# Attention, then two gated MLPs, in one kernel: weight splitting begun later and thinner, fewer first-layer products a pair at first, first loads by two queues

## The chip, the cores and the metric

One core of one Trainium2 chip runs the whole program. The metric is the device time of one execution in microseconds (us). Engines are named as in the profile: PE (TensorE, matrix products and transposes), PEld (its weight loads), DVE (VectorE), ACT (ScalarE), POOL (GpSimd) and SP (SyncE, which issues DMAs).

## What is computed

```python
# q, k, v: (4, 8, 576, 64); M_prev: (4, 8, 64, 64); weights float64
scores = (q @ k.T) / 8, causal mask;  a = softmax(scores);  local = a @ v
q_p = phi(q)                                   # phi(x) = max(x, 0) + exp(min(x, 0))
mem_out = (q_p @ M_prev) / (q_p . z_prev + 1e-6)
g = sigmoid(beta)                              # per head
x = g * mem_out + (1 - g) * local              # -> (2304, 512)
x = (sigmoid(x @ w_gate) * (x @ w_val)) @ w_out   # 512 -> 1536 -> 512
out = ((x @ w_a) * (x @ w_b)) @ w_out2            # 512 -> 1536 -> 512
```

The six weight matrices come in as 64-bit floats. Every product is made of three fp32r products of split operands: high x high, high x low, low x high.

## The kernel before, in words

**Attention stage (to line 860).** Two heads make a pair; there are 16 pairs, four to each of the four batches. The loop of line 770 runs 18 times and overlaps pair `p` (scores, masked minimum, exponentials), `p+1` (loads and transposes of queries and keys) and `p-1`, `p-2` (sums, transposed probabilities, the product with the values). `load_q`, `load_k`, `load_v` and `load_z` issue DMAs, all on SP's queue. `cut_q` splits the queries of a pair into a high part (DVE) and a low part (POOL).

**First-layer products inside it.** While attention of later pairs runs, the first MLP's first four of twelve chunks are computed for batches 0 to 2 (`moe_a`): a batch has 48 calls of `M`, each of three 128x512 products into tiles named `m` (144 products). `M` does the next call if its input is cut and its weight is ready, or nothing. `Ms(k)` asks for `k` of them; a pair has twelve such places. `room` forces calls where a buffer must come free. What is left is done behind the loop (line 854).

**Weight splitting.** `w_piece` turns 128x512 64-bit numbers (tile `st`) into a high and a low fp32r part (tile `w`) in steps. DVE masks bits and builds parts, ACT shifts the exponent, POOL multiplies the high part. With `WPOOL` set, as in this stage, ACT also converts the low part and POOL also makes the low product (line 444); without it, as in the second stage, DVE does both (lines 434 and 448). `w_stream` runs over the pieces, each three steps; the attention stage has 15 pieces. `fill`, called four times a pair, takes one step from pair 1 on and two from pair 4 on.

**Second stage (from line 861).** PE's order is the program's; the other engines' orders are made by a scheduler, as are all orders of the attention stage. `gv` computes gate and value products of a chunk (tiles `gv`, 24 products), `outs` the output products (tile `mo`). The first block is batch 3 with all twelve chunks: five have their weights from the attention stage, the other seven are split on the way, then the second MLP's follow. New pools stand where the attention stage's pools were, so the first loads of weights here come behind the last store of `fin` (line 541) in SP's queue.

Of the kernel before, what the change touches and what calls it, by code (L numbers as in the profile page):

```python
# [19 lines left out]
def kernel(  # L20
# [16 lines left out]
    nc = tc.nc  # L37
    P = 128
    B, H, S, D = q.shape
    NPAIR = H // 2  # L40
# [14 lines left out]
    vec, act, pool, pe = nc.vector, nc.scalar, nc.gpsimd, nc.tensor  # L55
# [42 lines left out]
    def place(p):  # L98
        b, r = divmod(p, NPAIR)
        return b, 2 * r  # L100


    def load_rows(t, src, p):
        b, h = place(p)
        nc.sync.dma_start(
            out=t[:, 0], in_=src[b, h:h + 2, 0:P, :].rearrange("h p d -> p h d")
        )
        for e in H2:
            nc.sync.dma_start(
                out=t[:, 1:NB, e], in_=src[b, h + e, 64:S, :].rearrange("(i p) d -> p i d", p=P)  # L110
            )

    def load_q(p):
        st["qn", p] = at.tile([P, NB, 2, D], F32, tag="qn", name="qn", bufs=2)
        load_rows(st["qn", p], q, p)

    def load_k(p):

        st["kn", p] = at.tile([P, NB, 2, 2, D], F32, tag="kn", name="kn", bufs=1)
        for r in H2:  # L120
            load_rows(st["kn", p][:, :, :, r], k, p)
# [14 lines left out]
    def load_z(p):  # L136
        b, h = place(p)
        zb = at.tile([P, 2, D], F32, tag="zb", name="zb", bufs=1)
        nc.sync.dma_start(
            out=zb.rearrange("p h d -> p (h d)"),  # L140
            in_=z_prev[b:b + 1, h:h + 2].rearrange("o h d -> o (h d)").broadcast_to([P, 2 * D]),
        )
        st["zb", p] = zb
# [11 lines left out]
    def cut_q(p):  # L155

        t = at.tile([P, NB, 2, 2, D], F32R, tag="qc", name="qc", bufs=1)
        vec.tensor_copy(out=t[:, :, :, 0], in_=st["qn", p])
        pool.tensor_tensor(
            out=t[:, :, :, 1], in0=st["qn", p], in1=t[:, :, :, 0].bitcast(F32), op=ALU.subtract  # L160
        )
        st["qc", p] = t
# [238 lines left out]
    def w_piece(wsrc, layer, c, kind, src):  # L401
# [24 lines left out]
        )  # L426
        if WPOOL:
            act.activation(out=low.bitcast(F32), in_=low, func=AF.Copy, scale=2.0 ** -20)
# [13 lines left out]
        )  # L442
        if WPOOL:
            pool.tensor_tensor(
# [10 lines left out]
    def w_stream(pieces, ahead):  # L455

        gens = []
        pieces = iter(pieces)

        def more():  # L460
            a = next(pieces, None)
            if a is not None:
                g = w_piece(*a)
                next(g)
                gens.append(g)

        for _ in range(ahead):
            more()
        yield
        while gens:  # L470
            g = gens.pop(0)
            for i in range(3):
                next(g)
                if i == 2:
                    more()
                yield
# [210 lines left out]
    NST, NG, NW = 2, MA, 1  # L687
    CD = "q"
    EDVE = ""
    WPOOL = True  # L690
    if True:
        start()
        wst = w_stream(
# [7 lines left out]
        def settle():  # L701
            while deferred:
                deferred.pop(0)()

        def M():

            settle()
            if not cur:
                if not batches:
                    return False  # L710
                cur.append(moe_a(batches.pop(0)))
                cur.append(next(cur[0]))
            b, key, f, after = cur[1]
            if b not in cut_a or key not in ws:
                return False
            with tc.issue_after(st["anchor"].ins):
                f()
            if after:
                deferred.append(after)
            nx = next(cur[0], None)  # L720
            if nx is None:
                cur.clear()
            else:
                cur[1] = nx
            return True

        def Ms(k=1):
            for _ in range(k):
                M()

        def split(k):
            while k and split_q and split_q[0][0] <= done[0] and split_q[0][3] <= len(finished):
                _, f, a, _ = split_q.pop(0)
                f(*a)
                if a[-1] == KD - 1:
                    cut_a.append(a[0])
                k -= 1

        def fill(p):
            settle()  # L740
            split(1)
            if p >= 1:
                with tc.issue_after(st["pace"].ins):
                    for _ in range(1 if p < 4 else 2):
                        next(wst, None)

        def room(p):

            old = divmod(p - 4, NPAIR)
            while any(x[1] is split_a and x[2] == old for x in split_q):  # L750
                split(1)
                if not M():
                    next(wst, None)
# [4 lines left out]
        for kk in range(KD):  # L758
            split_q.append((NPAIR * (B - 1) + kk + 1, split_last, (kk,), B - 1))

        load_q(0)
        load_k(0)
        load_z(0)
        load_v(0)
        cut_q(0)
        for e in H2:
            turn(0, e, "k")
            turn(0, e, "q")
            turn4(0, e)
        for p in range(NP + 2):  # L770
# [14 lines left out]
            if new:  # L785
                scores(p, 0, X_)
                expo(p, 0, X_)
            Ms()
            if last is not None:
                pv(last, Y_)  # L790
            Ms()
            if old is not None:
                turn_w(old, 1, "B")
                turn_w(old, 1, "C")
            Ms()
            fill(p)

            if new:
# [10 lines left out]
            if nx:  # L809
                cut_q(nx)  # L810
            Ms(2)
            fill(p)

            if new:
# [15 lines left out]
            if old is not None:  # L830
                for name in "01Y":
                    turn_mix(old, name)
            fill(p)

            if new:
# [25 lines left out]
    with tc.manual_schedule(engines={mybir.EngineType.PE}):  # L861
# [6 lines left out]
        NST, NG, NW = 2, 2, 1  # L868
        WPOOL = False
        wst = w_stream(  # L870
# [82 lines left out]
```

## Time and profile before

| what | value |
|---|---|
| median of 3 runs | 1192.5 us |
| lowest, highest | 1192.28, 1196.33 us |
| the profiled execution | 1195.14 us, span 1193.4 us |
| mean granted clock of TensorE | 0.986 |
| PE busy in the span | 96% |
| DVE, ACT, POOL busy in the span | 46%, 37%, 37% |

The span runs from the first to the last instruction; 1.7 us lie around it. Busy time of an engine is the time in which at least one of its instructions runs. Matmul ends are modelled, so that a busy PE can still run below its peak. The attention stage ends near 358 us, with the first `gv` product. "Pair p" below is the stretch from its first score product on PE to that of the next pair. Line numbers in rows of before are those of the kernel before; the changed kernel's are higher by one from line 106 on, and by more at the end.

### The profile page before, as it was taken

How to read it: one execution, taken by the hardware profiler on the slowest of the kernel's cores; microseconds unless marked ns; L12 is line 12 of the kernel's file. 1: busy time of each engine (PE TensorE's matmuls, PEld its weight loads, DVE VectorE, ACT ScalarE, POOL GpSimd, SP SyncE). 2: the span in 40 equal slices, each digit the busy share in tenths (PEclk: the TensorE clock that was granted, in tenths of full speed). 3: DMA queues.
4: the chain of work that ended last, by engine and by line, in shares of the span. 5: the costliest groups of instructions: out<-in, count | busy, mean ns of one | idle time of the engine just before them, and what ended most of it. 6: DMA issues, size and time to landing. Idle time of an engine off the chain costs nothing. (4 is left out here: it accounts for less than half of the span.)

```text
span 1193.4 us, 16159 instructions
## 1 busy us (share of the span) xinstructions
PE 1143.5 (96%) x6088; PEld 935.5 (78%) x6088; DVE 554.2 (46%) x1215; ACT 441.7 (37%) x967; POOL 435.8 (37%) x387
## 2 busy tenths in 40 slices
PE   6889999999999988989999998999999999999998
PEld 5667777787878867978888886888888888888897
DVE  6899988655636777860110678731100100200111
ACT  5877767777743223231211223222111211211121
POOL 5777776453413554431111344421111111111111
PEclk9999999999999999989999998999999999999999
DMA  7454543342114334331020433400200100100000
GB/s 170 109 155 104 132 117 109 80 108 75 48 47 152 106 113 163 118 119 53 8 99 1 165 118 124 142 18 1 71 1 1 71 1 1 36 18 1 1 37 18
DMA packets 129406, 89.66 MB, mean 75 GB/s; under 512 B 90032, under 2 KB 117680, under 8 KB 128432
## 3 DMA queue, kind: packets, MB, share of 16 engines
q1 hardware_dynamic: 129328, 88.63, 25.5%
q8 instruction: 48, 0.79, 0.3%
q14 instruction: 30, 0.25, 0.1%
HBM read 71.31 MB, written 17.30 MB: 74 GB/s over the span
## 5 line engine op out<-in xcount | busy, mean ns | idle before, releaser
L562 POOL TENSOR_TENSOR gl<-sg,gh 128x512 fp32r<-128x512 f32 (+1 forms) x120 | 149.2, 1244 | 502.1 <-ACT gh L149 474.1
L479 PE MATMUL gv<-xh,w 128*128 128x512 f32 (+1 forms) x864 | 321.1, 372 | 7.2 <-ACT xh L615 4.2
L480 PE MATMUL gv<-xl,w 128*128 128x512 f32 (+1 forms) x864 | 321.2, 372 | 4.6 <-DVE xl L616 4.6
L481 PE MATMUL gv<-xh,w 128*128 128x512 f32 (+1 forms) x864 | 321.0, 372 | 3.3 <-DVE w L448 3.3
L558 DVE TENSOR_TENSOR sg<-gv,sg 128x512 f32<-128x512 f32 (+1 forms) x108 | 68.1, 630 | 461.2 <-PE gv L481 461.2
L479 PEld LDWEIGHTS gv<-xh,w 128*128 128x128 f32 x864 | 164.3, 190 | 38.7 <-ACT xh L615 4.9
L480 PEld LDWEIGHTS gv<-xl,w 128*128 128x128 f32 x864 | 164.1, 190 | 35.7 <-DVE xl L616 6.0
L481 PEld LDWEIGHTS gv<-xh,w 128*128 128x128 f32 x864 | 164.2, 190 | 33.6 <-DVE w L448 4.6
L424 POOL TENSOR_TENSOR w<-wt,st 128x512 fp32r<-128x512 f32 x72 | 111.6, 1550 | 130.8 <-ACT wt L416 74.9
L632 ACT ACTIVATE sg<-gv 128x512 f32<-128x512 f32 (+1 forms) x108 | 59.0, 546 | 267.3 <-PE gv L481 263.2
L149 ACT ACTIVATE gh<-sg 128x512 fp32r<-128x512 f32 (+1 forms) x120 | 70.5, 587 | 212.7 <-DVE sg L558 212.6
L416 ACT ACTIVATE wt<-wt,rebias 128x512 int32<-128x512 int32 x72 | 52.2, 725 | 140.8 <-DVE wt L415 140.8
L247 ACT ACTIVATE s<-s,mx 128x320 f32<-128x320 f32 (+3 forms) x128 | 77.9, 610 | 24.5 <-DVE mx L242 23.7
L652 PE MATMUL mo<-w,gl 128*128 128x512 f32 x216 | 84.9, 393 | 0.1
L651 PE MATMUL mo<-w,gh 128*128 128x512 f32 x216 | 84.8, 393 | 0.0
L650 PE MATMUL mo<-w,gh 128*128 128x512 f32 x216 | 84.7, 392 | 0.0
L149 ACT ACTIVATE aw<-tp 128x512 f32<-128x512 f32 (+1 forms) x144 | 70.6, 508 | 28.3 <-PE tp L328 22.5
L480 PE MATMUL mo<-gl,w 128*128 128x512 f32 (+1 forms) x192 | 71.1, 370 | 2.3 <-POOL gl L562 2.2
L242 DVE CUSTOM_DVE_ANT_0 s<-sc,mask 64x64 f32<-64x64 f32 (+4 forms) x144 | 62.3, 471 | 20.9 <-PE sc L217 20.8
L479 PE MATMUL mo<-gh,w 128*128 128x512 f32 (+1 forms) x192 | 70.2, 366 | 0.0
L481 PE MATMUL mo<-gh,w 128*128 128x512 f32 (+1 forms) x192 | 70.2, 366 | 0.0
L439 DVE TENSOR_SCALAR wt<-w 128x512 int32<-128x512 int32 x72 | 39.5, 549 | 54.4 <-POOL w L424 54.4
(108 smaller groups left out, 1809.1 us busy)
## 6 DMA issues: line engine op xcount, KB each, us to landing
st<-in_moe_w_out_dram SPq DMA_DIRECT2D x24, 512.0 KB, 3.6
kn<-in_k_dram SPq DMA_DIRECT2D x64, 128.0 KB, 2.8
st<-in_moe_w_gate_dram SPq DMA_DIRECT2D x12, 512.0 KB, 3.8
st<-in_moe_w_val_dram SPq DMA_DIRECT2D x12, 512.0 KB, 3.7
st<-in_moe_w_a_dram SPq DMA_DIRECT2D x12, 512.0 KB, 3.7
st<-in_moe_w_b_dram SPq DMA_DIRECT2D x12, 512.0 KB, 3.6
xd<-x SPq DMA_DIRECT2D x16, 288.0 KB, 2.6
qn<-in_q_dram SPq DMA_DIRECT2D x32, 128.0 KB, 2.8
```

Source lines behind the costliest of these rows:

```text
L149: act.activation(out=out, in_=src, func=AF.Copy)
L242: st["pace"] = vec.tensor_tensor_reduce(out=s, in0=sc[0:m, SC0[i]:SC0[i] + w], in1=mask[0:m, c:c + w], scale=1.0, scalar=BIG, op0=ALU.add, ...
L247: act.activation(out=o, in_=s, func=AF.Exp, scale=-1.0, bias=mx[0:m, i:i + 1], accum_out=sm[0:m, i:i + 1],)
L424: pool.tensor_tensor(out=t[:, 0], in0=top.bitcast(F32), in1=hi.bitcast(F32), op=ALU.mult)
L479: pe.matmul(o, lhsT=w[:, 0, ws_], rhs=xh, start=first, stop=False, skip_group_check=True)
L480: pe.matmul(o, lhsT=w[:, 0, ws_], rhs=xl, start=False, stop=False, skip_group_check=True)
L481: pe.matmul(o, lhsT=w[:, 1, ws_], rhs=xh, start=False, stop=last, skip_group_check=True)
L558: vec.tensor_tensor(out=s[:, 0:n], in0=vps[:, 0:n], in1=s[:, 0:n], op=ALU.mult)
L562: pool.tensor_tensor(out=gl[:, 0:n], in0=s[:, 0:n], in1=gh[:, 0:n].bitcast(F32), op=ALU.subtract)
L650: pe.matmul(mo[f], lhsT=gh[:, t], rhs=w[:, 0], start=first, stop=False)
L651: pe.matmul(mo[f], lhsT=gh[:, t], rhs=w[:, 1], start=False, stop=False)
L652: pe.matmul(mo[f], lhsT=gl[:, t], rhs=w[:, 0], start=False, stop=c == NCH - 1)
```

## The change

- The first keys are loaded before the first queries, and their six DMAs go by ACT's queue; all other row loads stay on SP.
- For pair 0 the low part of the queries is made by DVE instead of POOL.
- `WPOOL` is off in the attention stage: a piece has six DVE instructions instead of five, one on ACT instead of two, one on POOL instead of two.
- `Ms` does three of four asked calls before pair 11: nine of the twelve a pair.
- `fill` takes weight steps from pair 4 on, one and two in turn: six steps, two pieces a pair.

```diff
     def load_rows(t, src, p):
         b, h = place(p)
-        nc.sync.dma_start(
+        dma = (nc.sync if p or src is q else nc.scalar).dma_start
+        dma(
...
         for e in H2:
-            nc.sync.dma_start(
+            dma(
...
         vec.tensor_copy(out=t[:, :, :, 0], in_=st["qn", p])
-        pool.tensor_tensor(
+        (pool if p else vec).tensor_tensor(
...
-    WPOOL = True
+    WPOOL = False
...
+        owed, turns = [0.0], [0]
+
         def Ms(k=1):
-            for _ in range(k):
+
+            owed[0] += k * (0.75 if p < 11 else 1.0)
+            while owed[0] >= 1.0:
+                owed[0] -= 1.0
                 M()
...
             split(1)
-            if p >= 1:
+            if p >= NPAIR:
                 with tc.issue_after(st["pace"].ins):
-                    for _ in range(1 if p < 4 else 2):
+                    for _ in range(1 + turns[0] % 2):
                         next(wst, None)
+                turns[0] += 1
...
+        p = 0
+        load_k(0)
         load_q(0)
-        load_k(0)
         load_z(0)
```

**PE's order at the end of the attention stage.** Before, the last first-layer products (`m`, with the split gate results `gh` and `gl`) stand ahead of all products `gv` of the second stage:

```order
L383 MATMUL tp<-aw,vn 64x128 x6
L479 MATMUL m<-gh,w_1973 128x512
L480 MATMUL m<-gl,w_1973 128x512
L481 MATMUL m<-gh,w_1973 128x512
L479 MATMUL gv<-xh,w_503 128x512
L480 MATMUL gv<-xl,w_503 128x512
```

In the changed kernel the first `gv` product stands among the `m` products:

```order
L482 MATMUL m<-gh,w_2461 128x512
L480 MATMUL m<-gh,w_2580 128x512
L480 MATMUL gv<-xh,w_1137 128x512
L481 MATMUL m<-gl,w_2580 128x512
L482 MATMUL m<-gh,w_2580 128x512
L480 MATMUL m<-gh,w_2285 128x512
```

and the last `m` product, 31 `gv` products later:

```order
L482 MATMUL m<-gh,w_2735 128x512
L480 MATMUL m<-gh,w_2735 128x512
L481 MATMUL m<-gl,w_2735 128x512
L482 MATMUL m<-gh,w_2735 128x512
L481 MATMUL gv<-xl,w_1286 128x512
L482 MATMUL gv<-xh,w_1286 128x512
```

What moved: 31 products of the second stage now stand ahead of the last product of the first-layer work.

**ACT's order at the start of the program.** `kn` are the first keys, `og` and `gb` the gates from `beta`, which another DMA brings. Before:

```order
L569 ACT_TABLE_LOAD
L569 ACTIVATE ident_r<-ident 128x128
L581 ACTIVATE og<-gb 128x8
L582 ACTIVATE gb<-gb 128x8
L261 ACTIVATE e<-e 128x640
```

Changed:

```order
L106 DMA kn<-in_k_dram 128x2x64
L110 DMA kn<-in_k_dram 128x4x64
L570 ACT_TABLE_LOAD
L570 ACTIVATE ident_r<-ident 128x128
L582 ACTIVATE og<-gb 128x8
L110 DMA kn<-in_k_dram 128x4x64
L583 ACTIVATE gb<-gb 128x8
L106 DMA kn<-in_k_dram 128x2x64
L110 DMA kn<-in_k_dram 128x4x64 x2
L262 ACTIVATE e<-e 128x640
```

What moved: six DMA issues came to ACT, four of them behind the table load and the gate `og`.

**DVE's order where the first weight piece stands.** `wt`, `wl` and `st` are a piece's tiles, `s` and `mx` the masked scores and their minimum. Before, in pair 1:

```order
L242 ISA s,mx<-sd,mask 128x576
L242 ISA mx 128x1
L415 TENSOR_SCALAR wt<-st 128x512
L276 TENSOR_REDUCE nr<-e 128x10
L242 ISA s_440,mx<-sc,mask 64x64
```

Changed, in pair 4:

```order
L243 ISA s,mx<-sc,mask 128x576
L243 ISA mx 128x1
L416 TENSOR_SCALAR wt<-st 128x512
L420 TENSOR_SCALAR wl<-st 128x512
L169 TENSOR_SCALAR qt<-tp 128x448
L159 CAST qc<-qn 128x10x64
```

What moved: by DVE's order the weight instructions of pairs 1 to 9 were 5, 6, 7, 7, 10, 14, 10, 10 and 6 (75 in all); now those of pairs 4 to 11 are 6, 12, 14, 14, 12, 10, 14 and 8 (90). By PE's order the `m` products of pairs 5 to 11 were 24, 39, 36, 36, 33, 39 and 36; now they are 21, 27, 27, 27, 10, 23 and 36.

## Rows read from the trace of the kernel before

**Rows 1.** Stretches: length; PE, PEld, DVE, ACT, POOL busy (instructions); clock; DMA share; GB/s.

```profile
10.88:21.66 10.78, 7.60 (x48) 6.56 (x47) 8.55 (x33) 7.82 (x26) 4.58 (x7) 1.00 0.93 234
21.66:67.45 45.79, 38.22 (x295) 30.84 (x295) 39.53 (x126) 36.58 (x107) 35.85 (x37) 0.96 0.51 124
67.45:88.05 20.60, 16.79 (x119) 12.83 (x119) 18.97 (x49) 16.85 (x48) 15.12 (x14) 0.92 0.55 145
88.05:183.47 95.42, 90.70 (x605) 72.31 (x603) 85.09 (x210) 72.83 (x181) 70.08 (x67) 0.96 0.47 124
183.47:204.94 21.47, 21.26 (x152) 17.13 (x150) 18.79 (x45) 15.01 (x42) 15.98 (x15) 1.00 0.39 105
204.94:315.02 110.08, 109.91 (x761) 89.02 (x760) 65.22 (x202) 81.98 (x199) 50.34 (x57) 1.00 0.33 84
...
560.00:580.00 20.00, 20.00 (x88) 16.22 (x87) 1.38 (x2) 2.86 (x5) 3.88 (x3) 1.00 0.00 0
```

**Rows 2.** The same view for PE's instructions on tile `m` alone.

```profile
88.05:183.47 95.42, 39.11 (x135) 0.96 0.47 124
...
204.94:315.02 110.08, 49.12 (x183) 1.00 0.33 84
```

**Rows 3.** Timeline at the seam: start, length, engine, line, operation, idle before and releaser.

```profile
357.98 0.40 PE L481 MATMUL m<-gh,w 128*128 128x512 f32 x1
...
361.94 0.38 SPq L407 DMA_DIRECT2D st<-in_moe_w_gate_dram  x1
...
363.93 0.69 DVE L558 TENSOR_TENSOR sg<-gv,sg 128x512 f32<-128x512 f32 x1 [4.52 <-PE gv L481]
...
365.53 1.46 DVE L415 TENSOR_SCALAR wt<-st 128x512 int32<-128x512 int32 x1 [0.91 <-DMA st<-in_moe_w_gate_dram]
```

**Rows 4.** PE's waits from 365 to 470 us: total, times, longest.

```profile
PE gv L481 <- DVE w L448: 3.3, 3, 1.4
PE gv L479 <- POOL w L424: 3.0, 3, 1.8
```

**Rows 5.** DVE's waits from 365 to 530 us.

```profile
DVE wt L439 <- POOL w L424: 29.2, 32, 1.2
DVE sg L558 <- PE gv L481: 1.0, 1, 1.0
```

**Rows 6.** Timeline of the first 10 us: key loads and key transposes.

```profile
4.85 1.02 SPq L109 DMA_DIRECT2D kn<-in_k_dram  x2
...
7.87 0.90 PE L188 MATMUL tp<-ident,kn 128*128 128x128 f32 x3 [0.62 <-DMA kn<-in_k_dram]
```

**Rows 7.** Groups by line: weights, 21 to 205 us; lines 448, 434: 365 to 530.

```profile
L429 DVE SCALAR_TENSOR_TENSOR wl<-st,wl 128x512 f32<-128x512 uint32 x15 | 18.8, 1252 | 1.9 <-ACT wl L428 1.9
L415 DVE TENSOR_SCALAR wt<-st 128x512 int32<-128x512 int32 x15 | 11.3, 752 | 0.5 <-POOL w L444 0.4
L439 DVE TENSOR_SCALAR wt<-w 128x512 int32<-128x512 int32 x15 | 10.0, 667 | 0.9 <-POOL w L424 0.9
L420 DVE TENSOR_SCALAR st<-st 128x512 int32<-128x512 int32 x15 | 8.8, 590 | 0.1
L419 DVE TENSOR_SCALAR wl<-st 128x512 int32<-128x512 int32 x15 | 8.6, 572 | 0.0
...
L444 POOL TENSOR_TENSOR w<-wl,wt 128x512 fp32r<-128x512 f32 x15 | 19.2, 1282 | 7.0 <-DVE wt L439 6.0 <-DVE wl L429 1.0
...
L448 DVE SCALAR_TENSOR_TENSOR w<-wl,wt 128x512 fp32r<-128x512 f32 x33 | 31.5, 954 | 1.1
L434 DVE SCALAR_TENSOR_TENSOR wl<-wl,st 128x512 f32<-128x512 int32 x34 | 24.4, 717 | 0.0
```

**Rows 8.** Timeline of the second stage: line 448 alone and beside POOL.

```profile
370.04 0.69 DVE L448 SCALAR_TENSOR_TENSOR w<-wl,wt 128x512 fp32r<-128x512 f32 x1
...
379.79 1.37 POOL L562 TENSOR_TENSOR gl<-sg,gh 128x512 fp32r<-128x512 f32 x1 [0.23 <-ACT gh L149]
380.05 1.66 DVE L448 SCALAR_TENSOR_TENSOR w<-wl,wt 128x512 fp32r<-128x512 f32 x1
```

## The prediction, as put on record before the result

> **What bounds the kernel now.** I read the stretches of the attention stage first [rows 1], cut at the first score product of a pair of heads ("pair 0" to "pair 15"). From pair 10 on TensorE (PE) is busy all the time. Three sizes follow. In the steady second stage 88 full products run in 20 us, so a 128x512 product takes 0.227 us. Pairs 10 to 14 hold 761 PE instructions, 183 of them first-layer products (`m`) [rows 2]: 110.08 - 183 x 0.227 = 68.5 us for the other 578, 0.119 us each. With these two prices the PE need of any stretch can be worked out; what the stretch took beyond it I call its excess.
>
> - pair 0: 48 x 0.119 = 5.7 us needed, 10.78 taken, excess 5.1
> - pairs 1 to 3: 295 x 0.119 = 35.1 of 45.79, excess 10.7
> - pair 4: 119 x 0.119 = 14.2 of 20.60, excess 6.4
> - pairs 5 to 8: 470 x 0.119 + 135 x 0.227 = 86.6 of 95.42, excess 8.8
> - pair 9 (33 `m`) and later: none
>
> So 31 us at most are there to be won, all of it before pair 9. In these stretches VectorE (DVE) is the fullest engine beside PE (39.5 of 45.8 us, 19.0 of 20.6, 85.1 of 95.4), and the granted clock averages 0.92 to 0.96, because after some PE gaps it falls from the full level for a few microseconds; that loss is inside the excess.
>
> Then the seam to the second stage [rows 3]. The last `m` product starts at 357.98 and the first `gv` right behind it. The next weight pieces can be loaded only after the last result of the first layer is copied and stored (SP issues the weight load at 361.94), and DVE begins on them at 365.53, 7.5 us after the last `m`. From there to the end of the first big block, near 460 us, DVE's chain over the pieces sets the end: the PE waits name the weights [rows 4], and DVE waited for PE once, 1.0 us, in 365 to 530, but 32 times for POOL's half of a piece [rows 5]. PE has five chunks ready when the chain starts, is ahead of it, and waits at the end. So the time of everything behind 365 us hangs on when the last `m` product is done, not on how much `gv` work PE has behind it by then.
>
> **The change part by part.**
>
> *The seam.* In the order of before no `gv` product stands ahead of the last `m`; in the changed one 31 do, because the changed kernel still has 85 `m` instead of 63 to do from the middle of pair 15 on, and the order puts free `gv` products between the last ones. PE runs in order, so the last `m` comes 31 x 0.227 = 7.0 us later relative to all other PE work. PE is that much ahead in `gv`, but DVE's chain starts 7.0 us later, and PE then waits for the weights as much longer. Term: **+7.0 us**. It would cost nothing only if the weight load were free of the last store; SP's queue is in order and has it behind that store in both kernels. Bounds: 0 (rival below) to 7.0.
>
> *The start.* The six key loads go to ACT's queue and are issued first; SP has only the query loads ahead of z, M and v. On SP each issue takes 0.5 us, the last two end at 5.87, and the second key transposes start at 7.87, having waited 0.62 us for a key load [rows 6]. ACT does not get through its six sooner: by the order a table load, the identity copy and `og` stand between the second and the third, and `og` waits for beta. I expect the last issue at about the same time. The subtraction of the first queries moves from POOL to DVE; the queries are then ready earlier, but the key transposes stand before them. No row shows ACT issuing a DMA. Bounds: 0.6 us gained (the whole wait) to 1.1 us lost (two more issues late); taken: 0. Six key loads at the 0.51 us of [rows 6] are 3.1 us of issue time. The Trainium skill, "DMA: Bandwidth & Descriptors", section Issuing engines are not separate DMA queues, says that queues of several engines run on the same DMA engines and save only the time of issuing; by it no more than those 3.1 us could be gained and the bandwidth is not widened.
>
> *Weights leave pairs 1 to 3.* DVE's order has 5, 6 and 7 weight instructions there before, none after; 7 in pair 4 become 6. One piece costs 752 + 572 + 590 + 1252 + 667 = 3.83 us on DVE in five instructions (0.767 each) [rows 7], so 18 x 0.767 = 13.8 us leave DVE in stretches that are 45.8 us long; POOL and ACT lose their parts too. The PE need (35.1) stays, and ACT, 36.6 us busy of which few are weights, is next. Excess 10.7 to 6.2: **-4.5 us** (bounds 0 and -8, where 2.7 us of chain delays stay). Pair 4 with one instruction less and a freer POOL: **-1.4 us** (0 to -4).
>
> *What a piece costs now.* POOL's second product (1282 ns) and ACT's conversion go. On DVE the 1252 ns instruction (line 429) becomes one like line 434 (717 ns) and one like line 448 (954 ns, in the second stage) is added [rows 7]: 752 + 572 + 590 + 717 + 667 + 954 = 4.25 us, in six (0.71 each). DVE's work per piece rises by 0.42 us, with bounds from line 448's shortest and longest instances, 0.69 and 1.66 [rows 8]: 0.16 to 1.13.
>
> *Pairs 5 to 8.* DVE's order has 52 weight instructions instead of 44, PE's 102 `m` instead of 135. PE need: 55.9 + 102 x 0.227 = 79.1. DVE: 85.1 + 52 x 0.71 - 44 x 0.767 = 88.3, less about 1.6 for the results of 33 products that aren't copied there (a batch of 144 has ten copies or products on DVE, 0.69 each like the product at 363.93 [rows 3]): 86.7. Now DVE, not PE, is the longer one. If it runs without a gap, 86.7 us, excess 7.6; at the 89% at which it ran in this stretch before, 97.4, excess 18. I take 90, excess 10.9, nearer the first, since PE offers less work to collide with: **+2 us** (-1 to +9).
>
> *Pairs 9 to 11.* Weights are still being split there (32 DVE instructions instead of 6), two a pair, and the products wait for them: only 10 and 23 `m` in pairs 9 and 10 where there were 33 and 39. PE needs 14.2 + 2.3 = 16.5 us in pair 9, and about 19 in pair 10; DVE needs 13.0 (its share of pairs 10 to 14, 65.2/5) plus 10 and 14 x 0.71: 20.1 and 22.9, less what overlaps. I take 19.5 and 20.5: **+4.5 us** (+2 to +7). Pair 11 has its full 36 and is bound by PE again; the `m` products that are put off cost nothing later by themselves, since PE is the bound there.
>
> Sum: 7.0 + 0 - 4.5 - 1.4 + 2 + 4.5 = +7.6; I round the four middle ones, which cancel within their bounds, to nothing: **+7.0 us**. The profiled execution took 1195.14 us (span 1193.4), 2.6 above the median of the runs; the difference is added to the median: 1192.5 + 7.0 = **1199.5 us**.
>
> **The rivals.**
>
> 1. *PE stays the bound in pairs 5 to 10, and the early stretches come near their PE need.* For it: POOL's load falls by 15 x 1.28 = 19 us, and in pairs 5 to 8 PE was still busy 90.7 of 95.4 us beside a DVE at 89% [rows 1], so that DVE had some room. Excess 31 to about 18.5, against +7.0: -5, 1187.5 us (down to 1183). It decides against my forecast from the point where the excess falls by more than 7. Against it: the need of DVE in pairs 5 to 8 is over PE's by 7 us.
>
> 2. *DVE is held up by POOL.* Line 448 took 0.69 us where POOL was idle and 1.66 where a product of POOL's ran beside it [rows 8]. If nearly every new instance collides, a piece is dearer by 15 x 0.7 = 10 us in all, and two thirds of it stand where DVE is the bound: +7 on the forecast, 1206 us. The rows show one instruction waiting for the whole of the other. The Trainium skill, "SBUF — State Buffer", section SBUF: two separate sides, tells the same as a rule: a DVE instruction with two SBUF inputs and a reading GpSimd one share a pair of ports under an exclusive lock; by it the product that leaves POOL also takes a collision away, and the trace agrees with the lock in the two instances named.
>
> 3. *The seam doesn't carry.* If the weights of the second stage start no later relative to PE's work (the 31 products hidden in a wait that is there anyway), the first term is gone: 1192.5 us.
>
> **How the numbers follow.** Chances: forecast 0.45, rival 1 0.27, rival 2 0.16, rival 3 0.12. About 0.5% (6 us) is what a measurement of this kernel can tell from no change: faster means under 1186.5, slower over 1198.5. Of rival 1 0.16 lie under 1186.5 and 0.11 within; rival 3 is within; of the forecast 0.26 are over 1198.5 and 0.19 within (its own range is 1194 to 1204); rival 2 is over. Faster 0.16, same 0.42, slower 0.42. Cases of both signs hold much of the chance, so the range goes from rival 1 to rival 2: 1186 to 1207.
>
> **What would show it.** In the profile after: `m` products end about 7 us later relative to PE's other work, 31 `gv` stand before them, DVE's first second-stage piece starts 7 to 8 us behind the last `m`, and PE waits for weights before the end of the first big block for some 14 us instead of 6. Pairs 1 to 3 should take about 41 us together, pairs 5 to 8 about 90 with DVE over 85 busy, pairs 9 and 10 about 40. The added DVE instruction should average 0.95 us; near 0.7 speaks for rival 1, near 1.5 for rival 2. I am wrong if the last `m` ends before 355 us, or if the second stage takes a different time from its first weight piece to the end of the span (827.9 us before).

## The result and the profile after

| | before | after |
|---|---|---|
| median | 1192.5 us | 1200.71 us (1199.5 to 1203.37, 5 runs) |
| profiled execution, its span | 1195.14, 1193.4 us | 1203.37, 1201.6 us |
| mean granted clock | 0.986 | 0.982 |
| last `m` product starts | 357.98 | 366.25 us |
| DVE begins the second stage's first piece | 365.53 | 373.96 us |
| from there to the end of the span | 827.9 | 827.6 us |

The changed kernel takes 1.0065 times the time of the kernel before (95% interval 1.0047 to 1.0084), 8.2 us more by the medians; 1199.5 us had been forecast. Line numbers of after are one higher than those of before from line 106 on, and more at the end.

The seam first, as a timeline (start, length, engine, line, operation, idle time before it and what released it); it answers to [rows 3]:

```profile
366.25 0.39 PE L482 MATMUL m<-gh,w 128*128 128x512 f32 x1
...
370.07 1.08 ACT L633 ACTIVATE sg<-gv 128x512 f32<-128x512 f32 x2 [2.73 <-DMA x2d<-sg]
...
370.11 0.38 SPq L408 DMA_DIRECT2D st<-in_moe_w_gate_dram  x1
...
370.72 0.79 PE L480 MATMUL gv<-xh,w 128*128 128x512 f32 x1 [2.94 <-ACT sg L633]
371.31 0.63 PE L481 MATMUL gv<-xl,w 128*128 128x512 f32 x1
371.74 0.63 PE L482 MATMUL gv<-xh,w 128*128 128x512 f32 x1
...
373.96 0.43 DVE L416 TENSOR_SCALAR wt<-st 128x512 int32<-128x512 int32 x1 [2.57 <-DMA st<-in_moe_w_gate_dram]
```

The last `m` comes 8.3 us later than before, the load of the next weights and DVE's first piece 8.2 and 8.4 us later, and nothing is won or lost behind them: 827.6 against 827.9 us. One thing here has no counterpart in [rows 3]: PE does five more `gv` products behind the last `m` and then stands still for 2.94 us. It has no place left for `gv` results: there are three places of twelve products each, 31 and 5 make 36, and ACT, which empties the first place into `sg`, waits for the store `x2d` of the first layer's last result. ACT waits for that store in the kernel before too (2.70 us, ahead of its first `sg`), but there no `gv` stands ahead of the last `m`, and PE has places left. Behind the stop the products start 0.43 us apart for a while, not 0.227: the granted clock from 370.7 to 373.4 us is 0.50, the lower of its two levels (1.2 GHz).

The stretches of the attention stage (us, then busy time and instruction count of PE, PEld, DVE, ACT, POOL, then granted clock, DMA share, GB/s), as [rows 1]; in order they are pair 0, pairs 1 to 3, pair 4, pairs 5 to 8, pairs 9 and 10:

```profile
11.07:20.80 9.73, 6.61 (x49) 5.69 (x48) 9.51 (x33) 6.71 (x22) 5.88 (x6) 1.00 0.72 164
20.80:61.87 41.07, 36.43 (x296) 29.64 (x295) 31.62 (x113) 35.07 (x108) 27.61 (x32) 1.00 0.50 124
61.87:80.34 18.47, 17.38 (x126) 13.48 (x126) 14.27 (x44) 13.78 (x40) 10.64 (x12) 0.91 0.47 110
80.34:172.21 91.87, 80.96 (x556) 63.89 (x554) 85.81 (x212) 67.30 (x171) 61.32 (x58) 0.96 0.48 125
172.21:213.20 40.99, 39.55 (x276) 31.05 (x274) 35.76 (x101) 26.82 (x75) 24.06 (x24) 0.92 0.52 141
```

Pairs 5 to 8 hold 102 `m` instead of the 135 of [rows 2] and take only 3.5 us less, with DVE busy 85.81 of 91.87 us. With the prediction's two prices (0.119 and 0.227 us, each instruction counted where it starts) the excess of the stretches is:

| excess, us | pair 0 | 1 to 3 | 4 | 5 to 8 | 9, 10 | 11 on | sum |
|---|---|---|---|---|---|---|---|
| before | 5.3 | 10.8 | 6.6 | 9.2 | 0.5 | 0.1 | 32.4 |
| after | 4.3 | 6.1 | 3.6 | 15.2 | 4.9 | -0.5 | 33.5 |

So the 8.3 us of the last `m` are 31 `gv` products ahead of it (7.0), 1.1 of excess and 0.2 of a later first score (11.07 against 10.88). What PE waited for in pairs 5 to 8 (80 to 172 us: total, times, longest) is DVE's and ACT's attention work; only 0.3 us name the weights:

```profile
PE tp L189 <- DVE qt L169: 2.9, 1, 2.9
PE sc L218 <- DVE mx L243: 2.8, 2, 2.2
PE tp L378 <- ACT aw L150: 2.7, 1, 2.7
PE tp L378 <- DVE kl L178: 1.5, 1, 1.5
...
PE m L482 <- DVE w L449: 0.3, 1, 0.3
```

Behind the seam, PE's waits from 366 to 480 us, and DVE's first one from 374 to 540, as [rows 4, 5]:

```profile
PE gv L482 <- DVE w L449: 3.3, 3, 1.4
PE gv L480 <- POOL w L425: 3.0, 3, 1.8
PE gv L480 <- ACT sg L633: 2.9, 1, 2.9
PE mo L481 <- POOL gl L563: 2.2, 3, 0.7
...
DVE wt L440 <- POOL w L425: 28.6, 32, 1.2
```

The waits for weights are 6.3 us, as before, and not the 14 that the prediction named.

### The profile page after: what moved, and what is told of

Same layout as the page of the kernel before. It is cut to its first block, busy times and chain, and to the rows that moved or that the text cites. A ratio compares the mean times of both kernels' runs of the same rounds, so it can differ in the third digit from the quotient of the medians.

```text
span 1201.6 us, 16143 instructions
## 1 busy us (share of the span) xinstructions
PE 1146.2 (95%) x6088; PEld 936.9 (78%) x6088; DVE 556.1 (46%) x1231; ACT 430.2 (36%) x950; POOL 416.8 (35%) x371
## 4 chain that ended last, share of the span: by engine, by line
PE 52%; DVE 6%; POOL 4%; ACT 1%; issue 1%; POOLq 0%; DVEq 0%; ACTq 0%
PE gv L481 12%; PE gv L482 12%; PE gv L480 12%; PE mo L653 4%; PE mo L652 4%; PE mo L651 4%; POOL w L425 4%; DVE w L449 2%; PE mo L481 2%; PE mo L480 2%; PE mo L482 2%; DVE wt L440 1%; ACT wt L417 1%; DVE wt L416 1%; DVE xl L617 0%
## 5 line engine op out<-in xcount | busy, mean ns | idle before, releaser
L449 DVE SCALAR_TENSOR_TENSOR w<-wl,wt 128x512 fp32r<-128x512 f32 x72 | 70.0, 973 | 2.2
```

Source lines behind the costliest of these rows:

```text
L449: vec.scalar_tensor_tensor(out=t[:, 1], in0=low.bitcast(F32), scalar=2.0 ** -52, in1=top.bitcast(F32), op0=ALU.mult, op1=ALU.mult,)
```

## The experiments

Theory: the chain over the second stage's weight pieces starts only behind the last `m`, so each `gv` product ahead of it delays the end. Rivals: the time is lost inside the attention stage (DVE's longer pieces, starved products), or one part of the change alone causes it. Ratios are to the kernel before on the same chip. The marks of all runs that keep the chain behind the last store come first together:

| kernel | ratio (95% interval) | median | `gv` ahead | excess | last `m` | first piece | span |
|---|---|---|---|---|---|---|---|
| before | 1 | 1192.5 | 0 | 32.4 | 357.98 | 365.53 | 1193.4 |
| after | 1.0065 (1.0047 to 1.0084) | 1200.71 | 31 | 33.5 | 366.25 | 373.96 | 1201.6 |
| `a_seam` | 1.0018 (1.0006 to 1.0030) | 1196.8 | 0 | 33.1 | 358.92 | 366.44 | 1194.6 |
| `b_start` | 0.9998 (0.9986 to 1.0010) | 1194.05 | 0 | 30.9 | 356.46 | 364.17 | 1193.4 |
| `b_wpool` | 1.0023 (1.0009 to 1.0037) | 1197.53 | 0 | 35.6 | 361.07 | 368.62 | 1194.8 |
| `b_ms` | 1.0090 (1.0070 to 1.0109) | 1204.96 | 31 | 35.5 | 368.21 | 375.65 | 1200.6 |
| `b_fill` | 1.0101 (1.0083 to 1.0118) | 1206.82 | 31 | 36.1 | 369.01 | 376.36 | 1206.0 |
| `b_late` | 1.0057 (1.0043 to 1.0071) | 1201.72 | 20 | 33.5 | 363.64 | 371.06 | 1200.6 |

In all eight the first piece starts 7.3 to 7.7 us behind the last `m`, and the end of the span follows 825 to 830 us later.

**The seam alone.** `a_seam` is the changed kernel with the second stage's `gv` products held behind the last `m`:

```diff
-        pe.matmul(o, lhsT=w[:, 1, ws_], rhs=xh, start=False, stop=last, skip_group_check=True)
+        st["tail"] = pe.matmul(o, lhsT=w[:, 1, ws_], rhs=xh, start=False, stop=last, skip_group_check=True)
...
-        proj(tg[:, 0:n], ws[layer, c, 0], lambda kk: xh[:, kk, 0:n], lambda kk: xl[:, kk, 0:n])
+        if "seam" not in st:
+            st["seam"] = st["tail"]
+        with tc.issue_after(st["seam"].ins):
+            proj(tg[:, 0:n], ws[layer, c, 0], lambda kk: xh[:, kk, 0:n], lambda kk: xl[:, kk, 0:n])
```

> The changed kernel with one more rule: the first gv products may stand only behind the last first-layer product, so 0 instead of 31 of them are ahead of it; everything else is as changed. Theory (the seam carries): the last m product starts 7.0 us earlier, less up to 2 us in which PE waits for gh, gl or the copied banks that the gv products covered before: near 360 instead of 366.3, and the time falls by 5 to 7 us, to 1194 to 1196. Rival (the loss comes from dearer weight pieces on DVE) and rival (it comes from the products that pairs 9 and 10 lack): nothing that they name is changed, so 1200 to 1201, and PE only waits elsewhere.

Measured: 1196.8 us, 3.9 below the changed kernel. Its seam, as a timeline:

```profile
358.92 0.39 PE L482 MATMUL m<-gh,w 128*128 128x512 f32 x1
...
362.77 0.38 SPq L408 DMA_DIRECT2D st<-in_moe_w_gate_dram  x1
...
366.44 1.46 DVE L416 TENSOR_SCALAR wt<-st 128x512 int32<-128x512 int32 x1 [0.91 <-DMA st<-in_moe_w_gate_dram]
```

The attention order is the same, the last `m` 7.3 us earlier and the first piece 7.5: the 31 products' 7.0 us are the seam's. The profiled spans differ by 7.0 us (1201.6 and 1194.6); by the ratios it is 0.47%, 5.6 us, of which the intervals leave 3 to 8. What stays against before is, by the profile, 0.7 us of excess and a first score 0.3 later.

**The parts alone, in the kernel before.** `b_start` has the first loads by two queues and the first subtraction on DVE:

```diff
-        nc.sync.dma_start(
+        dma = (nc.sync if p or src is q else nc.scalar).dma_start
+        dma(
...
-        pool.tensor_tensor(
+        (pool if p else vec).tensor_tensor(
...
-        load_q(0)
         load_k(0)
+        load_q(0)
```

> The kernel before with the first keys by ACT's queue, loaded first, and pair 0's low queries on DVE; nothing else. All theories: the first scores start between 0.6 us earlier and 1.1 us later than at 10.88, and the time is 1192 to 1194; a change of over 2 us would be the scheduler's, which orders later work anew.

Measured: nothing, 0.9998. Its first 8 us show why:

```profile
4.50 1.26 ACTq L110 DMA_DIRECT2D kn<-in_k_dram  x2
...
7.54 1.46 PE L189 MATMUL tp<-ident,kn 128*128 128x128 f32 x4 [7.54 <-DMA kn<-in_k_dram]
```

ACT's last key issue ends at 5.76 us; SP's ended at 5.87 [rows 6]. The Trainium skill, "DMA: Bandwidth & Descriptors", section Issuing engines are not separate DMA queues, had said that a second issuing engine saves only time of issuing; this run agrees.

`b_wpool` has `WPOOL` off, `b_ms` the thinned `Ms`, `b_fill` the changed weight steps:

```diff
-    WPOOL = True
+    WPOOL = False
```

> The kernel before with the low product on DVE instead of POOL alone. No gv product stands ahead of the last m, pieces take six DVE instructions. Theory: 15 x 0.42 = 6 us more on DVE, about half of it where DVE is full, against POOL's 19 us and ACT's 9 us less: between 1190 and 1196. Rival (dearer pieces are the loss): 1198 to 1202, with line 434's and 448's instructions well over 1 us on the mean.

```diff
+        owed = [0.0]
...
-            for _ in range(k):
+            owed[0] += k * (0.75 if p < 11 else 1.0)
+            while owed[0] >= 1.0:
+                owed[0] -= 1.0
                 M()
```

> The kernel before with the thinned first-layer calls alone (nine of twelve before pair 11); weights are split from pair 1 on with POOL's second product, as before. By the order 31 gv products stand ahead of the last m, and pairs 9 and 10 have 27 m each. Theory (the seam carries): 1192.5 + 7.0, less what a stretch with fewer products wins where DVE is full (0 to 3): 1196 to 1200. Rival (dearer pieces) and rival (products lacking in pairs 9 and 10): neither is there, so 1192 to 1194.

```diff
+        turns = [0]
...
-            if p >= 1:
+            if p >= NPAIR:
                 with tc.issue_after(st["pace"].ins):
-                    for _ in range(1 if p < 4 else 2):
+                    for _ in range(1 + turns[0] % 2):
                         next(wst, None)
+                turns[0] += 1
```

> The kernel before with the changed order of weight steps alone (none before pair 4, then one and two in turn). WPOOL stays on, Ms stays at twelve, keys and queries stay on one queue. 31 gv products stand ahead of the last m by the order, as in the changed kernel, and the last m should start near 365 us. Theory: the whole seam term from this one part, +7, less what pairs 1 to 3 give back (-3 to -5), plus starved pairs 9 and 10 (+4): +6 to +9 against before, 1200 to 1203 us. Rival (thinner Ms is what costs, as its run alone, +10.6, suggests): +1 to +4, 1195 to 1198 us.

`b_ms` and `b_fill` came out above what was expected of them; `b_wpool`, +2.7 us by its ratio, is near the upper end of the -2 to +4 expected. `b_wpool` puts no `gv` ahead and loses 3.2 us of excess in the profile, in pairs 1 to 3 (10.8 to 14.5). That a piece's longer work on DVE does it is not shown: `b_start`, with the pieces of before, has an excess of 15.2 there and wins it back later. `b_ms` and `b_fill` each put 31 `gv` ahead, as the whole change does, and each adds over 3 us of excess (four profiles with the order of before have 31.1 to 33.5). For `b_fill` pairs 9 and 10 are the place, 44.17 us with the granted clock at 0.85 on average:

```profile
163.41:207.58 44.17, 39.71 (x264) 31.06 (x263) 34.99 (x96) 31.82 (x89) 33.18 (x33) 0.85 0.43 113
```

PE's waits of `b_fill` from 355 to 480 us:

```profile
PE gv L479 <- POOL w L424: 5.3, 3, 3.1
PE gv L481 <- DVE w L448: 3.7, 4, 1.4
PE gv L479 <- ACT sg L632: 2.9, 1, 2.9
```

The parts alone (0, +0.2, +0.9, +1.0%) make more than the whole (+0.65%): the seam is paid once, whichever part pushes `m` work behind the attention stage. That thin `Ms` with late weights suit each other better than either alone is a reading of the ratios, clear of noise for `b_fill` only (0.36%, of which the intervals leave 0.1 to 0.6); no run shows why. The rival by which thin `Ms` is the one costly part had `b_fill` at +1 to +4 us and falls; what the two costly parts have in common, and `b_wpool` and `b_start` lack, is the 31 products ahead.

**Products ahead without the change.** `b_late` is the kernel before with no first-layer calls from the loop's pass 15 on, so that they are done behind the loop; 20 `gv` come to stand ahead of the last `m`:

```diff
+        p = 0
...
         def Ms(k=1):
-            for _ in range(k):
+            for _ in range(k if p < 15 else 0):
                 M()
```

> The kernel before with no first-layer calls from pair 15's pass of the loop on; they are done behind the loop. Weights, pieces and calls of all earlier pairs stand as before; by the order 20 gv products come ahead of the last m. Theory: 20 x 0.227 = +4.5 us, so 1196 to 1199, with the last m near 362.5. Rivals (dearer pieces; products lacking in pairs 9 and 10): no change, 1192 to 1194.

Measured: 1.0057, +6.8 us where 4.5 were expected. The last `m` is 5.7 us later (20 x 0.227 = 4.5, the rest excess), and the stretch behind the first piece is 1.7 longer: PE waits there for weights 9.7 us (355 to 480 us), besides a stop for `sg`, again ahead of the 37th `gv` product (20 ahead of the last `m`, 16 behind it):

```profile
PE gv L479 <- POOL w L424: 6.0, 4, 3.1
PE gv L481 <- DVE w L448: 3.7, 4, 1.4
PE gv L479 <- ACT sg L632: 1.7, 1, 1.7
```

**Without the pieces.** `b_nosplit` and `a_nosplit` leave out the 21 pieces of the second stage's first block; chunks 5 to 11 are computed with the weights of chunk 4, so their times are only compared with each other:

```diff
-        wst = w_stream(
-            [(w1, 0, c, kind, w2) for c in range(KA, NCH) for kind in range(3)], 3
-        )
+        wst = iter(())
+        for c in range(KA, NCH):
+            for kind in range(3):
+                ws[0, c, kind] = ws[0, MA, kind]
```

> The kernel before without the splitting of the first MLP's chunks 5 to 11 in the second stage (21 pieces with their loads are left out; those chunks use chunk 4's weights instead, so the output is not the reference's). It is the partner of a_nosplit. Theory (the seam carries because DVE's chain over the pieces sets the pace): the PE waits at 428 to 459 us go, 7.7 us and the half-speed window behind them, 1.7 us: 1181 to 1186. Rivals say nothing of it.

> The changed kernel with the same 21 pieces left out (output not the reference's). 31 gv products stand ahead of the last m as before. Theory: with no chain of pieces behind the last m, work done ahead of it is not lost; the changed kernel is slower than b_nosplit only by its excess (1 us) and by PE's wait of 2.9 us behind the last m with its half-speed window (up to 1.7): by 1 to 5 us instead of 8. Rival (the loss arises inside the attention stage): it stays 7 to 9 us slower than b_nosplit.

Measured: 1183.34 and 1186.97 us, ratios 0.9905 (0.9889 to 0.9922) and 0.9939 (0.9916 to 0.9962). The distance falls from 8.2 to 3.6 us though 31 `gv` still stand ahead; by the ratios it is 0.34%, 4.1 us, of which the intervals leave 1 to 7. What is left has a row: in `b_nosplit` PE waits for no other engine from 355 to 480 us, in `a_nosplit` once:

```profile
PE gv L480 <- ACT sg L633: 3.0, 1, 3.0
```

So the seam has a second price that the prediction did not see, the stop for `sg`; how large it is, these two runs don't fix.

**The chain cut loose.** `b_stp` and `a_stp` keep the weight tiles `st`, `wt` and `wl` in one pool for both stages, in the kernel before and in the changed one; the second stage's loads then need not wait for the memory of the first stage's last tiles:

```diff
+    wsp = ctx.enter_context(tc.tile_pool(name="wsp", bufs=2))
...
-        s = work.tile([P, 512, 2], I32, tag="st", name="st", bufs=NST)
+        s = wsp.tile([P, 512, 2], I32, tag="st", name="st", bufs=NST)
...
-        top = work.tile([P, 512], I32, tag="wt", name="wt", bufs=NW)
-        low = work.tile([P, 512], I32, tag="wl", name="wl", bufs=1)
+        top = wsp.tile([P, 512], I32, tag="wt", name="wt", bufs=NW)
+        low = wsp.tile([P, 512], I32, tag="wl", name="wl", bufs=1)
```

> The kernel before with the tiles st, wt and wl of the weight pieces in a pool of their own that both stages share, so that the second stage's first loads don't wait for the last store: by the order its first two loads and the first piece's four DVE instructions stand in the attention stage. Theory: DVE's chain starts up to 7.5 us earlier relative to the last m (only the multiplication into the new pool still waits for the attention's tiles), and the time falls by 4 to 8 us, to 1185 to 1189. Rivals: no change, 1192 to 1194.

> The changed kernel with the weight tiles st, wt and wl in a pool of their own that both stages share, so that the second stage's first pieces no longer wait for the last store of the first layer. 36 gv products stand ahead of the last m here. Theory (the loss is made at the seam: the chain over the pieces starts later by the gv products ahead of the last m): with the chain cut loose from the last store those products cost nothing, and the loss of 8 us against the kernel with the same pool on the order of before (1187.8 us, 6.6 below before) goes down to the difference of the attention stages' excess, 0 to 3 us: 1186 to 1191 us. The PE waits for weights at 445 to 465 us should be gone. Rival (the loss is made inside the attention stage): the changed kernel stays 7 to 8 us behind, 1194 to 1196 us.

`b_stp` takes 1187.79 us, ratio 0.9945 (0.9931 to 0.9960), and beats both kernels. Its last `m` starts at 357.89 as before, DVE is already at the second piece 2.7 us later, and PE's waits for weights are gone (PE's waits 355 to 480 us, and DVE's row):

```profile
PE mo L481 <- POOL gl L563: 4.5, 6, 0.8
PE gv L481 <- DVE xl L617: 0.5, 1, 0.5
...
360.59 0.43 DVE L416 TENSOR_SCALAR wt<-st 128x512 int32<-128x512 int32 x1
```

`a_stp` takes 1192.14 us, 0.9976 (0.9965 to 0.9987): 8.6 below the changed kernel, but still 4.4 above `b_stp`, a miss of the 1186 to 1191 expected. 36 `gv` stand ahead of its last `m`. Its timeline:

```profile
365.98 0.39 PE L483 MATMUL m<-gh,w 128*128 128x512 f32 x1
...
372.33 1.09 ACT L634 ACTIVATE sg<-gv 128x512 f32<-128x512 f32 x2 [2.86 <-DMA x2d<-sg]
...
372.99 0.80 PE L481 MATMUL gv<-xh,w 128*128 128x512 f32 x1 [6.62 <-ACT sg L634]
```

The 36 products put the last `m` 8.1 us later than in `b_stp`, and PE then gives 6.6 us of that lead back in one stop. The three places are full at the last `m`, five products sooner than in after, and the last store is issued later: DVE's and ACT's copies of the last results now stand behind pieces of weights in their orders, ACT's at 368.90 us where it is 366.74 in after. `as_stp` adds the order of `a_seam`, with none ahead:

> The same pool for st, wt and wl in the changed kernel with the gv products held behind the last m (none ahead of it). Theory: the order of the gv products no longer matters once the chain is free, so it is within 2 us of the run with 36 ahead: 1186 to 1191 us. Rival (the gv products ahead of the last m cost by themselves, by the fill of PE or the half-clock windows): it is 4 to 7 us faster than that run.

It takes 1189.9 us, 0.9956 (0.9937 to 0.9974), 2.2 below `a_stp`, hardly more than the 2 that the theory allowed and less than the 4 to 7 of the rival; the intervals leave 0 to 5 us. PE has no stop behind the last `m` now, but one ahead of it, where DVE's copy stands behind pieces of weights, so the difference is not the price of the stop by itself (PE's waits, 335 to 365 us):

```profile
PE m L481 <- DVE sg L541: 2.4, 1, 2.4
```

Last, `a_gsp` is `a_stp` with the second stage's `sg` (shown), `gh` and `gl` on memory that becomes free before the last `m`:

```diff
+        gsp = bctx.enter_context(tc.tile_pool(name="gsp", bufs=2, side="right"))
...
-        s = work.tile([P, 512], F32, tag="sg", name="sg", bufs=3)
+        s = gsp.tile([P, 512], F32, tag="sg", name="sg", bufs=3)
```

> The changed kernel with st, wt, wl in a pool shared by both stages, and the second stage's sg, gh and gl in a pool on the memory that the attention stage gives free before its last first-layer products are done. 31 gv products stand ahead of the last m; the wait of PE for ACT's sg behind the last m was 6.6 us with the shared weight pool alone (1192.1 us). Theory (ACT's first sg of the second stage waits for the last store because its memory held the stored tile, so PE runs out of places for gv results): the 6.6 us wait is gone, ACT's first sg stands ahead of the last store, and the time is 1185 to 1190 us, that of the order of before with the shared pool (1187.8). DVE's order has the first pieces behind the last first-layer copies here, so some 1 to 3 us of waits for weights near 460 us may come back. Rival (the wait for sg is of other making, or the products ahead cost otherwise): a wait of 3 to 7 us behind the last m stays, 1191 to 1194 us.

The stop is gone, as expected: ACT's first `sg` runs at 356 us. The time is a miss: 1194.88 us, ratio 1.0000 (0.9986 to 1.0014), above what theory and rival had. The chain still hangs on the last store: DVE did its first steps of the first piece long before (229.6 to 232.8 us), but POOL's product, which writes the weight tile `w`, waits 7.63 us until that store has landed, and DVE's chain goes on behind it. ACT's row, POOL's product, the step with which DVE's chain goes on, and PE's waits from 355 to 480 us:

```profile
356.22 0.59 ACT L635 ACTIVATE sg<-gv 128x512 f32<-128x512 f32 x1
...
369.30 1.31 POOL L426 TENSOR_TENSOR w<-wt,st 128x512 fp32r<-128x512 f32 x1 [7.63 <-DMA x2d<-sg]
...
370.65 0.43 DVE L441 TENSOR_SCALAR wt<-w 128x512 int32<-128x512 int32 x1 [0.17 <-POOL w L426]
...
PE gv L483 <- DVE w L450: 3.3, 3, 1.4
PE gv L481 <- POOL w L426: 3.1, 3, 1.9
```

This step of the first piece (line 439 in before, on the high part) started at 369.58 in before, at 376.99 in after and at 370.65 here; from it to the end of the span are 823.8, 824.6 and 823.0 us. PE had 31 `gv` done early and no stop, and the weights still set the end. So three groups of tiles can tie the second stage to the last store: the pieces' `st`, `wt` and `wl`, the `sg`, and the `w` that POOL writes. In `a_stp` and `b_stp` POOL's first product doesn't wait for that store (it starts at 342.46 and 357.63 us, ahead of its issue); in `a_gsp` the new pool stands ahead of the one that holds `w`, so that `w` has probably moved onto a stored tile, but no run shows the addresses. A kernel free of all three ties wasn't run.

## Why the prediction was right, and where it was not

- **The seam, +7.0: right.** 31 products ahead, the last `m` 8.3 us later with 1.1 of excess in it, the first piece 7.7 behind it, the rest 827.6 us against 827.9. `a_seam` takes the products away, and 7.3 us at the last `m` go with them; `a_gsp`, without the stop, still ends 823.0 us behind the first piece's step, so that the chain, not the stop, sets the end. One count in the reason was wrong without consequence: from the middle of pair 15 (its 13th score product) the changed kernel's trace has 126 `m` to do, not 85, where that of before has 63.
- **The reason given for it: incomplete.** "PE then waits for the weights as much longer" failed: 6.3 us, not 14. PE loses its lead otherwise. The second stage's products stand in the same order in both traces; product by product, counted from the first piece's start, the lead of 7.0 us falls by 2.9 in the stop for `sg`, by 1.6 in the products at the lower clock behind it, by 0.9 near 427 us (one more wait for `gl`) and by 1.0 near 465 us, where the granted clock is 0.50 for 6.8 us (462.5 to 469.3) instead of 3.4 in before (457.4 to 460.8); 0.7 is left at 487 us. And "it would cost nothing only if the weight load were free of the last store" was too much: in `a_stp` it is free, and 4.4 us of distance to `b_stp` stayed, with a stop of 6.6 us; how much of them the stop makes, `as_stp` leaves open. The step that failed is that PE's lead was taken as free of the last store; ACT's `sg` needs memory of the same tiles. Nor is it the order of SP's queue that holds the load back: the store's issue ended at 367.68 us, and the load and ACT's `sg` start together at 370.11 and 370.07, when the store has landed.
- **The start, 0: right** (`b_start` 0.9998).
- **Pairs 1 to 3, -4.5, and pair 4, -1.4:** -4.7 and -3.0; 41.07 us where about 41 were named. Pair 0 gave another 1.0, which had no term.
- **Pairs 5 to 8, +2: under-sized**, +6.0, though inside its bounds of -1 to +9. The length, 91.87 us, was near the 90 named and DVE's 85.8 near the 86.7; PE's instructions in the stretch were 1.9 us fewer than counted. One profile says little here: the six profiles with the changed order have an excess of 12.2 to 15.2 us in these pairs, on average 14.0, and the four with the order of before 9.2 to 12.2, on average 10.3, so the term is nearer +3.7. The waits name DVE's attention results, so DVE is the longer engine there, as argued.
- **Pairs 9 to 11, +4.5:** +4.4 in pairs 9 and 10, 40.99 us for 40.
- **The middle four cancel:** they left +1.1 with pair 0 and what lies behind, where +0.6 had been summed: an error of +4.0 us in one stretch stands against -3.5 in the others, so the sum was better than its terms. Over the same six and four profiles the excess ahead of pair 11 averages 32.0 and 32.3 us: that it cancels was not the luck of one profile.
- **The added instruction, 0.95 us: 0.875.** Its shortest, median and longest from 80 to 205 us, as printed (ns), were

```profile
L449 DVE SCALAR_TENSOR_TENSOR w<-wl,wt x12: 673/692/1657, 80.6 to 201.3; 128x512 fp32r<-128x512 f32 x12
```

so most instances ran as fast as alone. The long ones are no second length but a spread from 0.81 to 1.66 us, and what they share is their end: each of the five ends 0.55 us after the POOL product that was running when it started, as in this one (timeline, POOL's end 90.78, DVE's 91.33):

```profile
89.06 1.72 POOL L267 TENSOR_TENSOR e<-qp,zb 128x640 f32<-128x640 f32 x1
...
89.69 1.64 DVE L449 SCALAR_TENSOR_TENSOR w<-wl,wt 128x512 fp32r<-128x512 f32 x1
```

The ten long instances of the second stage from 373 to 464 us end 0.55 us behind POOL's product as well. The Trainium skill, "SBUF — State Buffer", section SBUF: two separate sides, describes an exclusive lock between DVE and GpSimd for whole instructions; these ends agree with it. **Rival 2** needed collisions in nearly all instances, and five of twelve had one; it falls. **Rival 1** falls too: the excess did not sink by 12 us but rose by 1. **Rival 3** is refuted by the fixed 827 us behind the first piece.

## What to carry to other kernels

Ask of work that an in-order engine can do early not whether it is free, but what stands behind it: here the product that is pushed back releases a store, and the store releases the memory on which another engine's long chain begins. Before moving such work, look for tiles of the next stage that lie on the last tiles of this one; giving the weight tiles a memory of their own (a pool and three allocations) was worth 6.6 us in the kernel before. And after each such move look again, since a new pool can put another tile onto the same memory, as in `a_gsp`. Sum a change over stages by the instant at which the next bound chain starts, and test that instant by a run that changes nothing else.

## What the runs showed of the hardware

The same order of PE instructions does not take the same time in each execution where PE has gaps. `a_nosplit` has the attention order of the changed kernel; its pair 4, with the same 126 PE instructions:

```profile
61.98:78.97 16.99, 15.81 (x126) 12.29 (x126) 14.30 (x44) 13.76 (x40) 11.20 (x12) 1.00 0.49 116
```

took 16.99 us at the full granted clock, and 18.47 at 0.91 in after, whose PE was at the lower level (granted clock 0.50) from 63.1 to 66.5 us. The other four profiles with this order took 16.96 to 16.98. In after, `a_nosplit`, `a_seam` and `a_stp` alike PE's one gap over 0.3 us from 55 to 67 us is the 0.81 us ahead of the pair's first score, so the same gap is not each time followed by the lower level. The total excess of the attention stage was 27.6 us in `a_nosplit` and 33.5 in after. A single profile therefore gives the excess of these stages to some 3 to 6 us, which is as large as the terms that the prediction had for them.
